# Convolution and gated two-layer network: small sums of the second layer moved between GpSimd, VectorE and DMA, and ScalarE's copies put in another order

## The chip, the core and the metric

The kernel runs on one core of a Trainium2 chip. Its engines are TensorE (PE in the profile, with PEld for its weight loads), VectorE (DVE), ScalarE (ACT), GpSimd (POOL) and SyncE (SP), each with an instruction queue of its own that is worked off in order. The metric is device time in microseconds of one execution; less is better.

## The reference

Everything is float32. A causal depthwise convolution of 7 taps over 8 sequences of 4096 tokens and 192 channels is followed by a network with 2048 hidden units and a gate:

```python
w = softmax(weight)                       # 8 heads x 7 taps
y[b, s] = sum_k w[h, k] * x[b, s - 6 + k] # 192 channels, 24 per head
h = y.reshape(32768, 192) @ w_in          # 192 x 2048
g = h * np.clip(h + 3.0, 0.0, 6.0) / 6.0
out = g @ w_out                           # 2048 x 192
```

## The kernel before

The 32768 tokens are worked off in 32 blocks of 1024. Block 0 is computed plainly at the start, together with the preparation of the weights; the other 31 run through the same two stages, `first_layer` and `second_layer`. All instructions stand in the order in which the program issues them (`tc.manual_schedule`).

**First layer.** 16 steps n = 0 to 15, two 64-row halves of TensorE's array side by side. `begin(n)` puts 12 matmuls into a slot of two PSUM banks, ScalarE scales the slot (L523), `end(n)` adds 6 matmuls, ScalarE writes relu to `g` (L302), and VectorE multiplies it with the slot (L306, a "gate"), which frees the slot. There are four slots, so `begin(n + 4)` needs gate n. Steps 0 to 7 give A11 and A22, steps 8 to 15 give A21 and A12: the tokens of a block and the hidden units are both cut in two, and these are the four quarters of the gated matrix, each 128 partitions x 8 chunks x 512 columns. Between the steps VectorE runs the convolution of a later block, `y += c[k] * x[k:]`, one instruction of 128x1536 for each tap k = 2 to 6 (L1056), before step 0 and after steps 1, 3, 5 and 7.

**Second layer.** It is a fast matrix multiplication with seven products on two levels. Level one uses the sums S3 = A11 - A21, S1 = A21 + A22 (in place of A21, by a DMA that adds, `add_pair`), S2 = S1 - A11 (in place of A11), and at the end S3 is rewritten as A12 - S2: ScalarE negates S2 into it (`negative`, L715), and a DMA adds A12. S3, S1 and the last rewriting go by pairs of chunks. Level two does the same within the products of A11, A22, A12 and S1: `small_sums` cuts a quarter into even and odd chunks and lower and upper 256 columns, x11, x12 (lower, even and odd) and x21, x22 (upper), and makes four small sums in the order 3, 2, 4 (each needs the one before it) and 1. Those of A11 lie in the tile `shared`, those of A22 in `sums4[0]` (z in the profile), those of S1 in `s5`. Form 1 of A11 and of A22 is made by two DMAs: one that copies x21 (SP's queue) and one that adds x22 (GpSimd's queue, `adding`).

The matmuls lie in four streams, one for each group of 32 columns of TensorE's array. `put` gives each a place on its stream's clock, 2 units for 512 columns and 1 for 256; each stream has 80 units. All other work of the stage gets a time on the same clock by `do(t, ...)`, and one sort by time gives the order of the program:

```python
        def do(t, fn, *args, **kw):
            streams[3].append((t - 0.5, lambda: fn(*args, **kw)))
...
        events = sorted(((t, fn) for st in streams for t, fn in st), key=lambda x: x[0])
```

So a time moved in `do` moves an instruction within its engine's queue; what it waits for is settled by the data alone. `level_two` runs one product's seven small products on one stream, in the order 1, then 6, 2, 7, 5, 4, 3, with ScalarE's copies between them (steps 1, 2, 6, 5, 7, 3 at L744 to L749): for the products of A22 on stream 2 and of A11 on stream 3 they take units 0 to 36, for that of S1 on stream 3 units 44 to 76. The rewritten S3 is used by streams 0 to 2 from unit 64 to 80, a pair of chunks every 4 units. `between` holds the preparation of the next block: `split_high` (L476), `split_low` and `split_mix` cut its convolved input into parts for the first layer.

Of the kernel before, what the change touches and what calls it, by code (L numbers as in the profile page):

```python
# [8 lines left out]
ALU = mybir.AluOpType  # L9
# [16 lines left out]
def kernel(  # L26
# [8 lines left out]
    nc = tc.nc  # L35
# [19 lines left out]
    NP = NC // 2  # L55
# [32 lines left out]
    for base, dma in ((0, nc.scalar), (D2, nc.sync)):  # L88
        dma.dma_start(
            out=w_sb[base : base + D2],  # L90
            in_=weight.unsqueeze(1).to_broadcast([H, GJ, KC]),
# [126 lines left out]
    for n in range(AHEAD):  # L218
# [8 lines left out]
        out=e_sb[:], in0=w_sb[:], in1=mx[:].to_broadcast([P, KC]), op=ALU.subtract  # L227
# [46 lines left out]
    A11, A21, A12, A22 = (g4[:, :, j] for j in range(4))  # L274
    S2, S1, S4 = A11, A21, A12
# [79 lines left out]
    every = range(NP)  # L355
# [3 lines left out]
    shared = ot.tile([P, NP, N], F32, name="shared")  # L359
# [97 lines left out]
    def add(out, x, y, op=ALU.add):  # L457
        nc.vector.tensor_tensor(out=out, in0=x, in1=y, op=op)
# [31 lines left out]
    y_own, y_other, pools, sums4 = [], [None], [], []  # L490
# [8 lines left out]
    def first_layer(i, jobs):  # L499

        slots = {}

        def both(n):
            return psum[:, 2 * slots[n] : 2 * slots[n] + 2]

        def mms(n, part, start=False, stop=False):
            group, c = divmod(n, NP)
            for s in range(K3):
                for k in range(2):
                    r = slice(k * D2, (k + 1) * D2)  # L510
                    nc.tensor.matmul(  # L511
                        out=psum[:, 2 * slots[n] + k], lhsT=r32(w_in_parts[part][r, c, s]),
                        rhs=r32(y_other[0][r, part, s] if group else y_own[part][r, s]),
                        start=start and s == 0, stop=stop and s == K3 - 1,
                        skip_group_check=True,
                    )

        def begin(n):
            slots[n] = free_slots.pop(0)
            mms(n, HIGH, start=True)  # L520
            mms(n, LOW)
            if n + 1 < count:
                nc.scalar.mul(both(n), both(n), 4097.0)  # L523
            else:
                lower, upper = (psum[:, 2 * slots[n] + k] for k in range(2))
                nc.scalar.mul(lower, lower, 4097.0)
                nc.vector.tensor_scalar(
                    out=upper, in0=upper, scalar1=4097.0, scalar2=None, op0=ALU.mult
                )

        def end(n):
            group, c = divmod(n, NP)
            mms(n, MIX, stop=True)
            to = g4[:, c, 1:3] if group else g4[:, c, 0::3]
            relu(to, both(n))
            gate(to, both(n))
            free_slots.append(slots[n])

        count = 2 * NP
        begin(0)  # L540
        begin(1)
        for job in jobs.get(-1, ()):
            job()
        for n in range(count):
            if n == count - 3:
                begin(n + 2)
            end(n)
            if n < count - 3:
                begin(n + 2)
            for job in jobs.get(n, ()):  # L550
                job()
            if n < NP and n % 2:
                small_sums(shared, A11, (3, 2, 4), nc.gpsimd, every[n - 1 : n + 1])
            if n in (3, NP - 1):
                r = slice(n - 3, n + 1)
                nc.sync.dma_start(out=four_parts(shared[:, r])[0], in_=four_parts(A11[:, r])[2])
            if n == NP - 1:
                sums4[:] = [pools[0].tile([P, NP, N], F32, name="z4", tag="own")]
                nc.sync.dma_start(out=four_parts(sums4[0])[0], in_=four_parts(A22)[2])
                small_sums(sums4[0], A22, (3,), nc.gpsimd)  # L560
                adding(four_parts(shared)[0], four_parts(A11)[3])
            if n == NP + 1:
                third_sum(0)
                add_pair(0)
                adding(four_parts(sums4[0])[0], four_parts(A22)[3])
            if n == NP + 3:
                third_sum(1)
                small_sums(sums4[0], A22, (2,), nc.gpsimd)
                add_pair(1)

    def adding(out, x):
        nc.gpsimd.dma_start(out=out, in_=x, accum_op=ALU.add)  # L572
# [8 lines left out]
    def third_sum(p, engine=nc.gpsimd):  # L581
        g_sums(engine, (3,), every[pair_of(p)], 2)
# [7 lines left out]
    def four_parts(x):  # L590
        return [x[:, c::2, t] for t in halves for c in range(2)]

    def small_sums(to, x, which, engine=nc.gpsimd, r=every):

        r = slice(r[0], r[-1] + 1)
        x11, x12, x21, x22 = four_parts(x[:, r])
        s1, s2, s3, s4 = four_parts(to[:, r])
        forms = {
            1: (s1, x21, x22, ALU.add), 2: (s2, x22, s3, ALU.subtract),
            3: (s3, x11, x21, ALU.subtract), 4: (s4, x12, s2, ALU.subtract),  # L600
        }
        for n in which:
            o, p, q, op = forms[n]
            engine.tensor_tensor(out=o, in0=p, in1=q, op=op)  # L604
# [17 lines left out]
    def second_layer(i, between):  # L622
        last = i + 1 == NB
        ours = [free_slots.pop(0) for _ in range(3)]
        x_, b, y_, c, a, _ = (psum[:, 2 * n + k] for n in ours for k in range(2))
        z = pools[1].tile([P, NP + 1, N], F32, name="z2", tag="other")
        sums2, p1 = z[:, 0:NP], z[0:DH, NP]
        ends = [psum[:, 2 * free_slots[0] + k] for k in range(2)] if last else [b, b]
        s5 = A22
        copy = nc.scalar.copy  # L630
        m = slice(0, DH)
        lo, hi = halves
        both = nc.sync, nc.scalar
        first, second, third, fourth = (rows(q) for q in range(4))
# [9 lines left out]
        clock = [0] * 4  # L644
# [5 lines left out]
        def do(t, fn, *args, **kw):  # L650
            streams[3].append((t - 0.5, lambda: fn(*args, **kw)))  # L651
# [87 lines left out]
        p4 = Fourth()  # L739

        def level_two(n, p, order, j=3):
            A, E, B, C = chains[j]
            steps = {
                1: lambda: copy(out=B, in_=A),  # L744
                2: lambda: copy(out=p()[first, lo], in_=A),
                6: lambda: copy(out=C, in_=B),
                5: lambda: copy(out=p()[second, lo], in_=E),
                7: lambda: copy(out=p()[second, hi], in_=C),
                3: lambda: copy(out=p()[first, hi], in_=C),  # L749
            }  # L750
            to = {1: A, 2: A, 6: B, 5: E, 7: C, 3: B, 4: C}
            for k in order:
                small(n, k, to[k], k in (1, 5), j)
                if k != 4:
                    do(clock[j], steps[k])

        rest = 6, 2, 7, 5, 4, 3
        chunks, first_fill = list(every), [True]
# [53 lines left out]
        assert clock == [80] * 4  # L812

        for t in halves:
            do(24 if t == hi else 20, copy, out=p4[third, t], in_=b[first, t])
        do(16, copy, out=p1[third], in_=b[second])
        do(20, copy, out=B2, in_=A2)
        do(31.9, copy, out=C2, in_=B2)
        do(32.2, copy, out=D2, in_=B2)
        do(12, copy, out=a[second], in_=a[fourth])  # L820
        do(28, copy, out=a[fourth], in_=a[second])
        do(40, lambda: copy(out=p2(second, hi), in_=C2))
        do(48, copy, out=a[second], in_=a[fourth])
        do(44, lambda: copy(out=p2(first, lo), in_=A2))
# [10 lines left out]
        do(7, small_sums, sums2, A12, (3, 2), nc.vector)  # L835
        do(7, small_sums, sums4[0], A22, (4,), nc.vector)
        do(7, small_sums, sums2, A12, (1,), nc.vector)
        for t, when in ((lo, 28.5), (hi, 32.5)):
            do(when, lambda t=t: add(S2[:, :4, t], S1[:, :4, t], A11[:, :4, t], ALU.subtract))
        do(33, small_sums, s5, S1, (3,), nc.vector)  # L840
        do(32, tiles)
        do(36, fold_with, p1)
        do(36.1, small_sums, s5, S1, (2,), nc.vector)
        do(36.2, g_sums, nc.vector, (2,), every[4:], 4)
        do(36.05, fold_with, p4, 2)
        do(38.7, copy, out=b[m], in_=p1)
        do(21, last_sum, sums2, A12)
        do(36.3, small_sums, s5, S1, (1, 4), nc.vector)
        for n, t in zip(range(0, NP, 2), (36.5, 40.5, 48.3, 50.5)):
            do(t, negative, slice(n, n + 2))  # L850
        do(45.5, lambda: copy(out=late["p7"], in_=c[m]))
        do(60.2, lambda: add(late["u3"], b[m], late["p7"]))
# [83 lines left out]
    with tc.manual_schedule():  # L936
# [4 lines left out]
            out=c_sb[:], in0=e_sb[:], in1=sm[:].to_broadcast([P, KC]), op=ALU.mult  # L941
# [14 lines left out]
        b = take()  # L956
# [62 lines left out]
        n = 3  # L1019
# [94 lines left out]
        for i in range(1, NB):  # L1114
            jobs = {n: [tap] for n, tap in zip((-1, 1, 3, 5, 7), taps)}
            jobs[-1] = left + jobs.get(-1, [])
            first_layer(i, jobs)
            def begin_conv():
                x_tiles[i + 2] = load_x(i + 2)
                conv[:] = conv_jobs(i + 2)  # L1120

            between, conv = [], []
            if i + 1 < NB:
                between += [(40, split_high), (57, split_low), (70, split_mix)]
                between += [
                    (t, lambda n=n: swap_parts(nc.gpsimd, (n,)))
                    for n, t in ((HIGH, 69), (LOW, 69), (MIX, 71))
                ]
            if i + 2 < NB:
                between += [(1, begin_conv), (58, lambda: conv[0]()), (62, lambda: conv[1]())]  # L1130
            left = second_layer(i, between)
            taps = conv[2:]
# [33 lines left out]
```

## Time and profile before

| | |
|---|---|
| median of 3 runs | 2264.55 us (2263.73 to 2266.02) |
| profiled execution | 2265.02 us, its span 2263.2 us |
| granted TensorE clock | 0.998 |
| TensorE busy | 2240.2 us (99%) |
| VectorE, ScalarE, GpSimd busy | 1938.1 us (86%), 1735.9 us (77%), 1292.1 us (57%) |
| DMA | 345.71 MB in 386540 packets, mean 153 GB/s |
| S1's adding DMAs (g<-g, L585) | 124 of 512 KB, median 6.6 us from issue to landing |
| S3's adding DMAs (s<-g) | 124 of 512 KB, median 5.6 us |
| the copies and adds of form 1 | shared<-g 62 of 256 KB by SP (2.5 us) and 31 of 512 KB by GpSimd (5.7 us); z<-g 31 of 512 KB by SP (3.2 us) and, with those of A12, 62 by GpSimd (7.3 us) |

Times in the timeline are microseconds from the start of the span. Lines of the timeline have start, length, engine, line of the program, operation, tiles (out<-in), shapes and count; an "x2" puts two instructions in a row together. What stands in brackets is the idle time before and what ended it. Spans on GpSimd are rough: an instruction can be shown as begun while the one before it still runs. The lines by stretches have, after the stretch and its length, the busy time and number of instructions of PE, PEld, DVE, ACT and POOL, then the granted clock, the DMA engines' share and GB/s. The block shown has its first layer from 1069.13 to 1102.10 and its second from 1102.10 to 1137.88; the next first layer follows until 1170.86.

### The profile page before, as it was taken

How to read it: one execution, taken by the hardware profiler on the slowest of the kernel's cores; microseconds unless marked ns; L12 is line 12 of the kernel's file. 1: busy time of each engine (PE TensorE's matmuls, PEld its weight loads, DVE VectorE, ACT ScalarE, POOL GpSimd, SP SyncE). 2: the span in 40 equal slices, each digit the busy share in tenths (PEclk: the TensorE clock that was granted, in tenths of full speed). 3: DMA queues.
4: the chain of work that ended last, by engine and by line, in shares of the span. 5: the costliest groups of instructions: out<-in, count | busy, mean ns of one | idle time of the engine just before them, and what ended most of it. 6: DMA issues, size and time to landing. Idle time of an engine off the chain costs nothing.

```text
span 2263.2 us, 55547 instructions
## 1 busy us (share of the span) xinstructions
PE 2240.2 (99%) x22984; PEld 1488.1 (66%) x22984; DVE 1938.1 (86%) x1890; ACT 1735.9 (77%) x2391; POOL 1292.1 (57%) x1064
## 2 busy tenths in 40 slices
PE   9999999999999999999999999999999999999997
PEld 6466666667666667666666666676666666666664
DVE  8888888888898888888888888888888889888875
ACT  7578787787877787877878777878778787777784
POOL 2466654566655666555666456665456655566643
PEclk9999999999999999999999999999999999999999
DMA  6388888988889878888887798787888878987776
GB/s 154 69 151 152 163 157 153 166 147 163 155 153 171 147 151 161 160 155 164 149 163 155 152 170 143 154 161 159 160 156 150 164 154 156 169 143 154 147 149 111
DMA packets 386540, 345.71 MB, mean 153 GB/s; under 512 B 213968, under 2 KB 298448, under 8 KB 386288
## 3 DMA queue, kind: packets, MB, share of 16 engines
q0 software_dynamic: 131344, 250.72, 62.1%
q1 hardware_dynamic: 253704, 91.18, 18.7%
q8 instruction: 180, 2.95, 0.5%
q14 instruction: 72, 0.59, 0.1%
q10 hardware_dynamic: 1240, 0.27, 0.1%
HBM read 31.72 MB, written 25.17 MB: 25 GB/s over the span
## 4 chain that ended last, share of the span: by engine, by line
PE 49%; POOL 16%; issue 12%; DVE 12%; DMA 7%; ACT 3%; POOLq 0%; SPq 0%; DVEq 0%; ACTq 0%
PE psum L654 25%; PE psum L511 20%; DVE g L306 7%; DMA s<-g 5%; DVE y L1056 4%; POOL s L414 4%; POOL g L572 3%; POOL z L604 2%; POOL s L572 2%; ACT g L302 2%; PE psum L296 2%; PE psum L341 2%; POOL shared L604 2%; POOL z L572 2%; DMA g<-g 1%
## 5 line engine op out<-in xcount | busy, mean ns | idle before, releaser
L654 PE MATMUL psum<-g,w_out 128*32 128x512 f32 (+1 forms) x5968 | 863.9, 505 | 7.0 <-DMA g<-g 6.1
L654 PE MATMUL psum<-s,w_out 128*32 128x512 f32 (+1 forms) x3024 | 765.9, 588 | 8.8 <-DMA s<-g 8.6
L306 DVE SCALAR_TENSOR_TENSOR g<-g,psum 128x1024 f32<-128x1024 f32 (+1 forms) x528 | 619.2, 1186 | 148.1 <-ACT g L302 147.7
L302 ACT ACTIVATE g<-psum,half 128x1024 f32<-128x1024 f32 (+1 forms) x528 | 565.2, 1087 | 5.9 <-PE psum L511 5.2
L511 PE MATMUL psum<-y_own,w_in 64*128 64x512 f32 x4464 | 523.4, 389 | 0.0
L511 PE MATMUL psum<-y_other,w_in 64*128 64x512 f32 x4464 | 516.0, 386 | 0.0
L654 PEld LDWEIGHTS psum<-g,w_out 128*32 128x32 f32 x5968 | 348.8, 109 | 243.0 <-issue 98.5
L523 ACT ACTIVATE psum<-psum 128x1024 f32<-128x1024 f32 x465 | 468.7, 1008 | 47.1 <-PE psum L511 44.9
L511 PEld LDWEIGHTS psum<-y_own,w_in 64*128 64x128 f32 x4464 | 413.5, 184 | 117.7 <-issue 26.0
L511 PEld LDWEIGHTS psum<-y_other,w_in 64*128 64x128 f32 x4464 | 418.1, 184 | 87.8
L604 POOL TENSOR_TENSOR shared<-g,shared 128x256 f32<-128x256 f32 x248 | 357.0, 1439 | 88.6 <-DVE g L306 57.1
L1056 DVE SCALAR_TENSOR_TENSOR y<-x,c_sb,y 128x1536 f32<-128x1536 f32 x186 | 335.3, 1803 | 1.5 <-ACT y L1054 1.3
L572 POOL DMA_DIRECT2D s<-g x124 | 149.4, 1264 | 283.2 <-PE psum L654 198.0
L654 PE MATMUL psum<-g,w_s 128*32 128x256 f32 x1488 | 288.3, 381 | 0.0
L654 PEld LDWEIGHTS psum<-s,w_out 128*32 128x32 f32 x3024 | 194.6, 109 | 79.2 <-DMA s<-g 19.8
L654 PE MATMUL psum<-z,w_s 128*32 128x256 f32 x992 | 232.1, 382 | 0.0
L654 PE MATMUL psum<-z,w_out 128*32 128x256 f32 x992 | 204.4, 380 | 0.0
L604 POOL TENSOR_TENSOR shared<-g 128x256 f32<-128x256 f32 x124 | 91.9, 741 | 188.6 <-DVE g L306 188.6
L414 POOL TENSOR_TENSOR s<-g 128x1024 f32<-128x1024 f32 x62 | 195.8, 3158 | 0.0
L572 POOL DMA_DIRECT2D g<-g x124 | 180.1, 1466 | 17.9 <-POOL s L414 9.1
L572 POOL DMA_DIRECT2D z<-g x62 | 94.6, 1525 | 144.7 <-ACT z L575 133.8
L651 ACT COPY psum<-psum 32x512 f32<-32x512 f32 (+1 forms) x186 | 82.9, 446 | 122.0 <-PE psum L654 118.0
(116 smaller groups left out, 2874.3 us busy)
## 6 DMA issues: line engine op xcount, KB each, us to landing
y_other<-y_own POOLq DMA_DIRECT2D x180, 384.0 KB, 8.1
g<-g POOLq DMA_DIRECT2D x124, 512.0 KB, 6.6
s<-g POOLq DMA_DIRECT2D x124, 512.0 KB, 5.6
z<-g POOLq DMA_DIRECT2D x62, 512.0 KB, 7.3
out_dram<-shared SPq DMA_DIRECT2D x378, 64.0 KB, 5.4
x<-in_x_dram SPq DMA_DIRECT2D x53, 388.5 KB, 5.7
shared<-g SPq DMA_DIRECT2D x62, 256.0 KB, 2.5
z<-g SPq DMA_DIRECT2D x31, 512.0 KB, 3.2
```

The lines of the kernel that those rows point to most:

```text
L296: nc.tensor.matmul(out=psum[:, b], lhsT=w[r], rhs=src, start=start, stop=stop, skip_group_check=onto,)
L302: nc.scalar.activation(r6, h, ACT.Relu, bias=half[:], scale=1.0 / 6.0)
L306: nc.vector.scalar_tensor_tensor(out=g_, in0=g_, scalar=1.0, in1=h, op0=ALU.min, op1=ALU.mult)
L341: lambda p=p: nc.tensor.matmul(out=bank[j * QS : (j + 1) * QS, tokens], lhsT=w_out[:, p, w, cols], rhs=x[:, p, tokens], start=(first and p ...
L414: engine.tensor_tensor(out=o[:, r], in0=a[:, r], in1=b[:, r], op=op)
L511: nc.tensor.matmul(out=psum[:, 2 * slots[n] + k], lhsT=r32(w_in_parts[part][r, c, s]), rhs=r32(y_other[0][r, part, s] if group else y_own[ ...
L523: nc.scalar.mul(both(n), both(n), 4097.0)
L572: nc.gpsimd.dma_start(out=out, in_=x, accum_op=ALU.add)
L604: engine.tensor_tensor(out=o, in0=p, in1=q, op=op)
L651: streams[3].append((t - 0.5, lambda: fn(*args, **kw)))
L654: nc.tensor.matmul(out=out, lhsT=w, rhs=x, start=start, stop=True, tile_position=(0, j * QS), skip_group_check=True,)
L1056: jobs.append(lambda k=k: nc.vector.scalar_tensor_tensor(out=y[:], in0=x[:, :, k : k + N], scalar=c_sb[:, k : k + 1], in1=y[:], op0=ALU.mu ...
```

## The change

1. First layer, GpSimd: form 1 of A11 is summed with the other three, for each pair of steps, and form 1 of A22 after step 9. The two SP copies and the two GpSimd adding DMAs that made them are dropped.
2. First layer: S3's first pair is summed by VectorE after gate 9, no longer by GpSimd.
3. Second layer, VectorE: chunks 4 and 5 of S2 are summed in two halves behind chunks 0 to 3 (times 28.6 and 32.6); only chunks 6 and 7 stay in one sum at 36.1, now ahead of form 2 of S1.
4. Second layer, ScalarE and GpSimd: the four negations with their adding DMAs go from times 36.5, 40.5, 48.3 and 50.5 to 35.6, 36.6, 41 and 45, and `split_high` from 40 to 48.4.
5. Second layer, ScalarE: seven copies that nothing needs soon go later: step 2 of the products of A11 and A22 from 20 to 28.1, the three copies out of bank b from 16, 20 and 24 to 25.5, 29 and 30, and one within bank a from 28 to 34.

```diff
             if n < NP and n % 2:
-                small_sums(shared, A11, (3, 2, 4), nc.gpsimd, every[n - 1 : n + 1])
-            if n in (3, NP - 1):
-                r = slice(n - 3, n + 1)
-                nc.sync.dma_start(out=four_parts(shared[:, r])[0], in_=four_parts(A11[:, r])[2])
+                small_sums(shared, A11, (3, 2, 4, 1), nc.gpsimd, every[n - 1 : n + 1])
             if n == NP - 1:
                 sums4[:] = [pools[0].tile([P, NP, N], F32, name="z4", tag="own")]
-                nc.sync.dma_start(out=four_parts(sums4[0])[0], in_=four_parts(A22)[2])
                 small_sums(sums4[0], A22, (3,), nc.gpsimd)
-                adding(four_parts(shared)[0], four_parts(A11)[3])
             if n == NP + 1:
-                third_sum(0)
+                third_sum(0, nc.vector)
                 add_pair(0)
-                adding(four_parts(sums4[0])[0], four_parts(A22)[3])
+                small_sums(sums4[0], A22, (1,), nc.gpsimd)
...
                 if k != 4:
-                    do(clock[j], steps[k])
+                    do(clock[j] + (8.1 if k == 2 and n != 5 else 0), steps[k])
...
         for t in halves:
-            do(24 if t == hi else 20, copy, out=p4[third, t], in_=b[first, t])
-        do(16, copy, out=p1[third], in_=b[second])
+            do(30 if t == hi else 29, copy, out=p4[third, t], in_=b[first, t])
+        do(25.5, copy, out=p1[third], in_=b[second])
...
-        do(28, copy, out=a[fourth], in_=a[second])
+        do(34, copy, out=a[fourth], in_=a[second])
...
-        for t, when in ((lo, 28.5), (hi, 32.5)):
-            do(when, lambda t=t: add(S2[:, :4, t], S1[:, :4, t], A11[:, :4, t], ALU.subtract))
+        for r, t, when in (
+            (slice(0, 4), lo, 28.5), (slice(4, 6), lo, 28.6),
+            (slice(0, 4), hi, 32.5), (slice(4, 6), hi, 32.6),
+        ):
+            do(when, lambda r=r, t=t: add(S2[:, r, t], S1[:, r, t], A11[:, r, t], ALU.subtract))
...
-        do(36.1, small_sums, s5, S1, (2,), nc.vector)
-        do(36.2, g_sums, nc.vector, (2,), every[4:], 4)
+        do(36.1, g_sums, nc.vector, (2,), every[6:], 2)
+        do(36.2, small_sums, s5, S1, (2,), nc.vector)
...
-        for n, t in zip(range(0, NP, 2), (36.5, 40.5, 48.3, 50.5)):
+        for n, t in zip(range(0, NP, 2), (35.6, 36.6, 41, 45)):
             do(t, negative, slice(n, n + 2))
...
-                between += [(40, split_high), (57, split_low), (70, split_mix)]
+                between += [(48.4, split_high), (57, split_low), (70, split_mix)]
```

## The prediction

> **What bounds the kernel now.** I read the page first, then the stretches of one steady block, then the timeline of VectorE and GpSimd in that block, the waits of TensorE's weight loads, and last the timeline of ScalarE.
>
> ```profile
> PE 2240.2 (99%) x22984; PEld 1488.1 (66%) x22984; DVE 1938.1 (86%) x1890; ACT 1735.9 (77%) x2391; POOL 1292.1 (57%) x1064
> ```
>
> The stretches of the two stages (after the length: busy time and instructions of PE, PEld, DVE, ACT, POOL):
>
> ```profile
> 1069.13:1102.10 32.97, 32.97 (x292) 26.83 (x288) 27.74 (x25) 30.90 (x32) 24.10 (x20) 1.00 0.75 159
> 1102.10:1137.88 35.78, 35.78 (x434) 19.78 (x432) 32.23 (x33) 23.24 (x43) 16.75 (x15) 1.00 0.96 157
> ```
>
> TensorE is the bound. A block is a first layer (32.97 us in every block) and a second layer (35.78 here; the blocks' period averages 69.3, so 36.3 on average). The first layer is 16 steps of 2.04 us without a gap. The second has four column groups ("streams") of 80 units each. In the timeline one unit takes 0.4293 us, so 34.4 us is its floor: at most 1.9 us per block, 58 us in all, can be won there. I placed each of its matmuls against start + 0.4293 × unit; the means of 29 blocks show where the streams fall behind: stream 3 is 0.97 late from unit 4, streams 2 and 3 are 1.22 late from unit 28, stream 3 is 1.46 late from unit 52, and all are about 2.0 late from unit 76. The waits of the weight loads (us in total, times, longest; a stretch of 29 blocks) name the causes of three: S1's first pair (unit 4), ScalarE's copies of step 7 (unit 28) and S3's negated pairs (unit 76).
>
> ```profile
> PEld psum L654 <- DMA g<-g: 22.6, 29, 1.4
> PEld psum L654 <- DMA s<-g: 16.7, 26, 1.3
> PEld psum L654 <- ACT z L748: 14.5, 29, 0.5
> ```
>
> At unit 52 the cause is ScalarE's copy of step 1 (L744, 1125.29 to 1125.63).
>
> The first layer has no wait, but VectorE has no slack there either. Start, length, engine:
>
> ```profile
> 1146.29 1.81 DVE L1056 SCALAR_TENSOR_TENSOR y<-x,c_sb,y 128x1536 f32<-128x1536 f32 x1
> 1148.02 2.43 DVE L306 SCALAR_TENSOR_TENSOR g<-g,psum 128x1024 f32<-128x1024 f32 x2
> 1150.38 1.81 DVE L1056 SCALAR_TENSOR_TENSOR y<-x,c_sb,y 128x1536 f32<-128x1536 f32 x1
> ```
>
> ```profile
> 1146.52 2.18 POOL L604 TENSOR_TENSOR shared<-g,shared 128x256 f32<-128x256 f32 x1 [1.32 <-DVE g L306]
> 1148.78 0.74 POOL L604 TENSOR_TENSOR shared<-g,shared 128x256 f32<-128x256 f32 x1
> 1149.48 0.74 POOL L604 TENSOR_TENSOR shared<-g 128x256 f32<-128x256 f32 x1
> ```
>
> A tap and two gates fill each 4.08 us. The GpSimd sum issued during a tap takes 2.18 us where its neighbours take 0.74: it ends 0.60 after the tap. The reverse is in the next lines: VectorE's sum of S3 takes 2.30 where it takes 1.21 alone (so in all 22 that I matched with a running GpSimd sum), because GpSimd's sum runs until 1106.68; 1.21 + 1.21 - 0.12 = 2.30.
>
> ```profile
> 1105.47 2.30 DVE L414 TENSOR_TENSOR s<-g 128x1024 f32<-128x1024 f32 x1
> ```
>
> ```profile
> 1103.32 3.36 POOL L604 TENSOR_TENSOR z<-g,z 128x1024 f32<-128x1024 f32 x1
> ```
>
> So a VectorE instruction with two SBUF inputs and a GpSimd sum exclude each other, whole instruction by whole instruction. Gates, which read PSUM, are not held (1.22 with GpSimd busy, 1.21 without).
>
> **The change in the first layer.** Form 1 (x21 + x22) of A11 moves to GpSimd: one more 128x256 sum per pair of steps, priced by the row of form 3 at 0.74, or 0.70 from start to start. Two SP copies and two GpSimd adding DMAs per block vanish. GpSimd then wants, from a tap's end T: form 2 to T+0.60, form 4 from T+0.68, form 1 from T+1.38, and the next pair's form 3 from T+2.08 to T+2.82. The next tap comes at T+2.28 (1150.38 against 1148.10). In before, form 3 was over 0.16 before it; now it is in its way for 0.54. No tap of before started on a running GpSimd sum (0 of 116), so this price lies between 0 and 0.54; I take 1.81 + 0.54 - 0.12 = 2.23, because the 22 sums follow it. Each pair then takes VectorE 4.51 instead of 4.08, and the second, third and fourth of the four taps end 0.42, 0.86 and 1.30 late.
>
> The Trainium skill, "SBUF — State Buffer", section "SBUF: two separate sides", says the pair of ports that VectorE and GpSimd share is locked for the whole instruction by whichever started first. By that rule the small sums hold the taps and the time is my sum; if only sums as long as those in the trace did, it would be the first rival's. The 22 waits agree with the rule.
>
> What TensorE loses: step m+4 starts in the PSUM slot that gate m frees. Gate 4 ends at 1153.31 and step 8 starts at 1153.76, 0.45 later, the same for the other even steps, 1.27 for odd ones; about 0.07 of this is latency (0.05 lie between the end of a copy, 1115.11, and the matmul that waits for it, 1115.16). Lateness of 0.42, 0.86, 1.30 against 0.38 leaves TensorE 0.04, then 0.48, then 0.92 late.
>
> S3's first pair moves to VectorE, behind gate 9. There it meets GpSimd's 2.41 us sum for A22 (form 3, L560): that one starts 2.08 after the last tap's end, the new VectorE sum is issued at 2.40. It waits 2.09, takes 1.21 + 2.09 - 0.12 = 3.18, and gate 10 ends 3.64 later than before. Against a slack of 1.27 - 0.07 + 0.92, step 14 waits 1.51 more. First layer: 32.97 + 0.92 + 1.51 = 35.4, +2.43 per block. The last block has no taps and keeps its time. Bounds: 2.0 to 2.8.
>
> Queued behind: S1's first pair (add_pair(0)) is issued by GpSimd after that sum, some 6 us before the second layer starts instead of 2.7. It landed 5.2 after its issue, so the wait at unit 4 goes even if the landing takes 2 us more. GpSimd's later sums end by 2.4 into the second layer, so VectorE's third pair there is no longer held and S1's last pairs land up to 1 us earlier. S2's pieces of 128x512 cost 0.69 each (row of 96x512; between 0.42 and 1.22), wait for S1's third pair and hide before the last pair's landing (15.4 us after the second layer's start in before), for which S1's small sums wait anyway; without that cover they would cost VectorE 1.4 and TensorE nothing, since S2's last chunks are wanted at unit 56, 24.0 us in.
>
> **The change in the second layer.** Postponing five copies before unit 28 (four of 0.36 and one of 0.58) lets step 7's copies end at 11.2 after the start instead of 13.0; unit 28 is at 12.0, so that wait goes. Then ScalarE is the limit:
>
> ```profile
> 1119.25 0.37 ACT L749 COPY z<-psum 32x256 f32<-32x256 f32 x1
> 1119.52 1.05 ACT L575 ACTIVATE s<-g 128x1024 f32<-128x1024 f32 x1
> 1120.60 0.59 ACT L651 COPY psum<-z 96x512 f32<-96x512 f32 x1
> 1121.21 0.36 ACT L822 COPY shared<-psum 32x256 f32<-32x256 f32 x1
> 1121.60 1.49 ACT L476 ACTIVATE y_own<-y 128x1536 fp32r<-128x1536 f32 x1
> 1122.99 1.05 ACT L575 ACTIVATE s<-g 128x1024 f32<-128x1024 f32 x1
> 1123.94 0.34 ACT L824 COPY shared<-psum 32x256 f32<-32x256 f32 x1
> 1124.29 0.36 ACT L825 COPY shared<-psum 32x256 f32<-32x256 f32 x1
> 1124.68 0.59 ACT L851 COPY shared<-psum 96x512 f32<-96x512 f32 x1
> 1125.29 0.34 ACT L744 COPY psum<-psum 32x256 f32<-32x256 f32 x1
> ```
>
> S3's first negation now runs ahead of the L749 copies, which so end at 17.5 as in before, though TensorE is there 1.2 earlier. From there to L744 come negations two, three and four (3 × 1.05) and copies of 0.59, 0.36, 0.34, 0.36 and 0.59: 5.4 us, and with L744 23.2. Before it was 5.8 and 23.5, with split_high's 1.49 in place of two negations. Unit 52 (22.32) waits until 23.2: stream 3 is 0.87 late instead of 1.46. The copy into bank b makes streams 0 to 2 wait 0.2 to 0.5 at unit 44, less than that. The negations' adding DMAs go through GpSimd's queue, which sat idle for 2.0 to 4.9 us between them in before. The last negation goes out at 22.1 instead of 26.0, and its landing (7.5 in before) at 29.6 is 3 us ahead of unit 76: that 0.54 goes. Gain: 2.0 - 0.87 = 1.13 per block; bounds 0.5 (an ACT queue 0.6 longer) to 1.7 (lateness of 0.3).
>
> **Sum.** 30 × 2.43 = 73 lost, 30 × 1.13 + 2 for the last block = 36 gained. The profiled execution took 2265.0 (span 2263.2 and 1.8 around it), 0.5 above the median of 2264.55. 2264.5 + 37 = 2301.5 is the median that I expect. With the bounds, 2275 to 2334.
>
> **Rivals.** First, faster: the sums never get ahead of a tap, and GpSimd falls behind instead. It decides on 0.20 us: form 3 of the second pair is issued at 1150.18, the tap at 1150.38. Then S3's first pair meets a 0.74 sum at most and gate 10 ends 0.85 late, within its 1.20; the first layer stays at 33.0. The wait at unit 4 may stay, but its 0.97 lies beside unit 52's 0.87, so some 33 are gained: 2232. For it: no tap was ever held. Against it: the two engines' mutual waits above, and that a tap and four sums (1.7 + 2.8) exceed 4.08. Second: the taps are held, but S3's first pair gets in ahead of the 2.41 us sum (0.32 us decide). Then only 0.92 is lost: 30 × 0.92 - 36 = -8: 2257, between 2241 and 2277 by the bounds of the second layer. Third: GpSimd runs two sums in a row before a waiting tap gets its turn, and each of three taps waits 0.7 more: 30 × 2.1 = 63 more, 2365; nothing in the trace shows it.
>
> **How the numbers follow.** My forecast 0.65, the first rival 0.15, the second 0.13, the third 0.05, others 0.02. The range from 2245 to 2334 takes in the forecast with its bounds and nearly all of the second rival and leaves 0.2 out. A measurement of this kernel tells about 0.2% (4.5 us) from no change. Faster: the first rival and two thirds of the second, 0.24; same 0.07; slower 0.69.
>
> **What would show it.** Right: a first layer of about 35.4 us and a second of about 35.2; taps of 2.2 us; a VectorE sum at L414 of about 3.2 behind gate 9; no wait for DMA g<-g at unit 4 or DMA s<-g at unit 76. Wrong: taps still at 1.81 and a first layer of 33.0, or a second layer whose lateness at unit 52 is not ScalarE's.

## The result and the profile after

The changed kernel takes 2327.3 us (2325.49 to 2328.69) beside 2264.1 us before: a ratio of 1.0277, 95% interval 1.0259 to 1.0295. It is 63 us slower. The prediction said 2301.5, slower with a chance of 0.69, and a range of 2245 to 2334. The profiled execution took 2328.69 us, with a span of 2326.9.

The first line of the profile's page of the kernel after, to be held against that of before:

```profile
PE 2266.4 (97%) x22984; PEld 1474.6 (63%) x22984; DVE 2031.7 (87%) x1983; ACT 1738.2 (75%) x2391; POOL 1292.0 (56%) x1126
```

VectorE has 93 instructions and 94 us more, GpSimd 62 instructions more and the same busy time; DMA moves 280.66 MB instead of 345.71. Then the stretches of one block of the kernel after, first and second layer (stretch, length, busy time and count of PE, PEld, DVE, ACT, POOL, clock, DMA share, GB/s):

```profile
1099.69:1134.94 35.25, 34.01 (x290) 26.53 (x289) 31.65 (x26) 30.87 (x32) 25.93 (x23) 1.00 0.52 112
1134.94:1171.09 36.15, 35.87 (x434) 19.52 (x432) 31.60 (x35) 23.34 (x43) 14.79 (x15) 1.00 0.79 133
```

From the first matmul of one layer to that of the next, as a mean over the blocks, before has 32.97 and 36.33 us, after has 35.26 and 36.16. So the first layer loses 2.29 per block and the second wins only 0.17; 30 × 2.12 = 64 is the whole difference.

The waits of the weight loads in the kernel after (what waited for what: us in total, times, longest):

```profile
PEld psum L511 <- DVE g L306: 79.2, 113, 1.6
...
PEld psum L649 <- ACT psum L646: 21.4, 29, 0.7
PEld psum L649 <- ACT shared L740: 21.4, 28, 0.8
PEld psum L649 <- ACT psum L739: 16.1, 29, 0.6
```

The first line is new: TensorE's first-layer steps wait for gates. The waits for S1's first pair, for S3's pairs and for step 7's copies, which led this list before, are gone. In their place stand three waits for ScalarE (L646, L739 and L740 are L651, L744 and L745 of before), at units 44, 52 and 64.

Now one first layer of the kernel after. VectorE's timeline (start, length):

```profile
1116.52 2.26 DVE L1054 SCALAR_TENSOR_TENSOR y<-x,c_sb,y 128x1536 f32<-128x1536 f32 x1
...
1125.51 3.26 DVE L414 TENSOR_TENSOR s<-g 128x1024 f32<-128x1024 f32 x1
```

GpSimd's timeline beside it:

```profile
1115.72 1.45 POOL L599 TENSOR_TENSOR shared<-g 128x256 f32<-128x256 f32 x2
...
1125.29 2.40 POOL L599 TENSOR_TENSOR z<-g 128x1024 f32<-128x1024 f32 x1
1129.07 1.24 POOL L567 DMA_DIRECT2D g<-g  x1 [1.38 <-DVE s L414]
```

The first GpSimd line is form 1 and the next pair's form 3. They run until 1117.17, and the tap shown at 1116.52 takes 2.26 instead of 1.81. The second is A22's sum: it began 0.22 ahead of VectorE's sum for S3, which then takes 3.26. GpSimd's end, 1127.69, plus VectorE's own 1.23 is 1128.92; the sum ends at 1128.77. The last line issues the DMA for S1's first pair, 5.9 us before the second layer starts.

### The profile page after: what moved, and what is told of

Read it like the earlier page. It is cut to its first block, busy times and chain, and to the rows that moved or that the text cites. A ratio compares the mean times of both kernels' runs of the same rounds, so it can differ in the third digit from the quotient of the medians.

```text
span 2326.9 us, 55119 instructions
## 1 busy us (share of the span) xinstructions
PE 2266.4 (97%) x22984; PEld 1474.6 (63%) x22984; DVE 2031.7 (87%) x1983; ACT 1738.2 (75%) x2391; POOL 1292.0 (56%) x1126
## 2 busy tenths in 40 slices
DMA packets 320570, 280.66 MB, mean 121 GB/s; under 512 B 211489, under 2 KB 232481, under 8 KB 320321
## 4 chain that ended last, share of the span: by engine, by line
PE 40%; DVE 25%; ACT 24%; issue 10%; DMA 0%; POOL 0%; SPq 0%; DVEq 0%; ACTq 0%
PE psum L649 25%; DVE g L306 14%; PE psum L511 11%; DVE y L1054 8%; ACT s L570 5%; ACT g L302 3%; ACT psum L646 3%; ACT psum L523 2%; DVE y_own L1077 2%; ACT y L1052 2%; PE psum L296 2%; PE psum L341 2%; ACT y_own L476 2%; ACT shared L646 1%; ACT shared L740 1%
## 5 line engine op out<-in xcount | busy, mean ns | idle before, releaser
L649 PE MATMUL psum<-s,w_out 128*32 128x512 f32 (+1 forms) x3024 | 721.5, 589 | 0.0
L306 DVE SCALAR_TENSOR_TENSOR g<-g,psum 128x1024 f32<-128x1024 f32 (+1 forms) x528 | 604.8, 1180 | 73.0 <-ACT g L302 72.7
L511 PE MATMUL psum<-y_other,w_in 64*128 64x512 f32 x4464 | 546.2, 393 | 38.4 <-DVE g L306 35.2
L1054 DVE SCALAR_TENSOR_TENSOR y<-x,c_sb,y 128x1536 f32<-128x1536 f32 x186 | 372.1, 2000 | 1.5 <-ACT y L1052 1.4
L599 POOL TENSOR_TENSOR shared<-g 128x256 f32<-128x256 f32 x248 | 179.9, 742 | 179.6 <-DVE g L306 179.6
L649 PE MATMUL psum<-z,w_out 128*32 128x256 f32 x992 | 227.3, 379 | 0.0
L567 POOL DMA_DIRECT2D g<-g x124 | 166.6, 1362 | 82.0 <-DVE s L414 82.0
L266 POOL DMA_DIRECT2D y_other<-y_own x90 | 48.0, 534 | 284.4 <-issue 264.9
L649 PEld LDWEIGHTS psum<-g,w_s 128*32 128x32 f32 x1488 | 132.5, 109 | 98.3 <-ACT shared L740 22.1
L649 PEld LDWEIGHTS psum<-s,w_out 128*32 128x32 f32 x3024 | 179.4, 109 | 21.2
L646 ACT COPY psum<-psum 32x512 f32<-32x512 f32 (+1 forms) x186 | 82.9, 446 | 124.3 <-PE psum L649 121.1
```

The lines of the kernel that those rows point to most:

```text
L266: dma.dma_start(out=to[D2:P], in_=part[0:D2])
L306: nc.vector.scalar_tensor_tensor(out=g_, in0=g_, scalar=1.0, in1=h, op0=ALU.min, op1=ALU.mult)
L511: nc.tensor.matmul(out=psum[:, 2 * slots[n] + k], lhsT=r32(w_in_parts[part][r, c, s]), rhs=r32(y_other[0][r, part, s] if group else y_own[ ...
L649: nc.tensor.matmul(out=out, lhsT=w, rhs=x, start=start, stop=True, tile_position=(0, j * QS), skip_group_check=True,)
L1054: jobs.append(lambda k=k: nc.vector.scalar_tensor_tensor(out=y[:], in0=x[:, :, k : k + N], scalar=c_sb[:, k : k + 1], in1=y[:], op0=ALU.mu ...
```

## Experiments

All were compared with the kernel before on the same chip. The last two columns are the mean lengths of first and second layer, as above.

| kernel | us | ratio to before, 95% | first | second |
|---|---|---|---|---|
| before | 2264.1 to 2265.9 | | 32.97 | 36.33 |
| after | 2327.3 | 1.0259 to 1.0295 | 35.26 | 36.16 |
| e1_first_only | 2306.7 | 1.0165 to 1.0196 | 35.27 | 35.44 |
| e2_second_only | 2285.2 | 1.0072 to 1.0102 | 32.97 | 37.04 |
| e3_sum_gpsimd | 2301.8 | 1.0145 to 1.0176 | 33.78 | 36.81 |
| e4_form1_dma | 2276.4 | 1.0035 to 1.0069 | 33.51 | 36.30 |
| e5_a22_behind | 2284.8 | 1.0075 to 1.0105 | 33.76 | 36.23 |
| e6_y_later | 2313.3 | 1.0200 to 1.0230 | 35.26 | 35.69 |
| e9_old_second | 2241.0 | 0.9879 to 0.9908 | 32.97 | 35.47 |
| e8_best | 2227.6 | 0.9821 to 0.9854 | 32.97 | 35.14 |
| e11_neg_only | 2326.9 | 1.0260 to 1.0294 | 35.26 | 36.24 |
| e10_split_earlier | 2213.7 | 0.9761 to 0.9790 | 32.97 | 34.67 |

**The two halves of the change.** e1_first_only is the kernel before with the first layer's part of the change (points 1 and 2 of the list above) and nothing else; e2_second_only is the kernel after with that part undone.

> The kernel before with the first layer's part of the change alone (all small sums of A11 and A22 on GpSimd, third_sum(0) on VectorE); the second layer stays as before. Theory A (GpSimd's sums and VectorE's sums hold each other): the first layer is 2.28 us longer per block as in the kernel after, taps 2.2 us and third_sum(0) 3.2 us; the wait at unit 4 goes and part of the one at unit 76, worth 0.2 to 0.7 a block: 2312 to 2326. Rival, the loss of the kernel after sits in the second layer's new order: near 2264 or below it.

> The kernel after with the first layer of before; S2 in pieces and the new order of ScalarE's copies stay. Theory A: the first layer is back at 33.0 us, the wait at unit 4 (0.97 us) is back, but later waits of 1.2 and 1.7 us on ScalarE set the lag anyhow: 2256 to 2264. Rival, the gain that the prediction gave to the second layer (1.13 a block) is there when the first layer doesn't disturb it: about 2230.

The halves add up: in the first layer +2.30 and 0, in the second -0.89 and +0.71, together -0.18 where the kernel after shows -0.17. So the first-layer half makes the first layer longer and the second shorter, since S1's first pair lands before it is wanted: no wait for it is left in e1_first_only. The reordering of the second layer is a loss by itself, some 20 us. For e1 the first layer came as expected, but the time lies 5 us below the range, because the second layer gains 0.89 per block where I had put 0.2 to 0.7. For e2 neither theory held: I had thought that the wait at unit 4 would be covered by the later waits for ScalarE, and it was not. Measured against start + 0.4293 × unit, the most delayed stream of e2 is late by 0.97 from unit 4, 1.39 from unit 44, 2.07 from unit 52 and 2.56 from unit 64; in the kernel after by 0.05, 0.52, 1.20 and 1.68. Nearly the same steps come on top of the lateness that is there. ScalarE is late too in e2: `split_high`, which matters at unit 64, starts 24.8 us into the stage, in the kernel after 24.0.

**What in the first layer costs 2.29.** Three kernels, each the kernel after with one edit. e3_sum_gpsimd:

```diff
-                third_sum(0, nc.vector)
+                third_sum(0)
```

> The kernel after with S3's first pair (third_sum(0)) back on GpSimd. Theory A: the taps are still held by GpSimd's sums (2.2 us), so about 0.7 us a block is left of the 2.28, and the S1 pair lands some 2 us later, which may cost 0.2 to 0.5 at unit 4: 2279 to 2293. Theory B (VectorE is simply full, and its added 1.2 us sum is the loss): the whole loss but what the second layer gains goes, about 2259.

e4_form1_dma:

```diff
-                small_sums(shared, A11, (3, 2, 4, 1), nc.gpsimd, every[n - 1 : n + 1])
+                small_sums(shared, A11, (3, 2, 4), nc.gpsimd, every[n - 1 : n + 1])
+            if n in (3, NP - 1):
+                r = slice(n - 3, n + 1)
+                nc.sync.dma_start(out=four_parts(shared[:, r])[0], in_=four_parts(A11[:, r])[2])
...
                 small_sums(sums4[0], A22, (3,), nc.gpsimd)
+                adding(four_parts(shared)[0], four_parts(A11)[3])
```

> The kernel after with A11's first small sums (form 1) taken by a copy and an adding DMA again, as before; the A22 sum on GpSimd and third_sum(0) on VectorE stay. GpSimd begins A22's sum about 2.3 us earlier, so that third_sum(0) meets less of it. Theory A (exclusion, the form-1 sums get in ahead of a tap): the taps are 1.8 us again and their lateness (0.7) goes, third_sum(0) falls from 3.26 to some 2.5: first layer 33.4 us, 2265 to 2280. Theory B (VectorE's added sum alone): no change from after, 2327.

e5_a22_behind:

```diff
-                small_sums(sums4[0], A22, (3,), nc.gpsimd)
             if n == NP + 1:
                 third_sum(0, nc.vector)
                 add_pair(0)
+                small_sums(sums4[0], A22, (3,), nc.gpsimd)
                 small_sums(sums4[0], A22, (1,), nc.gpsimd)
```

> The kernel after with GpSimd's form-3 sum of A22 (2.4 us) issued behind add_pair(0) instead of just before VectorE's third_sum(0). Theory A (third_sum(0) is long because it meets that sum): third_sum(0) takes 1.2 us again, step 14's wait of 1.5 us goes, only the taps' lateness of 0.7 is left in the first layer (33.7 us): about 2280. Theory B (VectorE's added 1.2 us is the loss, wherever GpSimd is): no change, 2327.

The groups of the taps and of VectorE's S3 sums (L414; after "|" busy time and mean ns of one) tell them apart. First e4_form1_dma:

```profile
L1058 DVE SCALAR_TENSOR_TENSOR y<-x,c_sb,y 128x1536 f32<-128x1536 f32 x186 | 335.2, 1802 | 1.5 <-ACT y L1056 1.4
L414 DVE TENSOR_TENSOR s<-g 128x1024 f32<-128x1024 f32 x93 | 148.6, 1625 | 1.1
```

Then e5_a22_behind:

```profile
L1054 DVE SCALAR_TENSOR_TENSOR y<-x,c_sb,y 128x1536 f32<-128x1536 f32 x186 | 371.8, 1999 | 1.5 <-ACT y L1052 1.3
```

Without form 1 on GpSimd, every tap is as before (1802 ns; 1803 before) and steps 8, 10 and 12 start on time; with it they stay held (1999; 2000 in the kernel after). The sum for S3 behind gate 9 takes what is left of A22's sum in front of it, in VectorE's timelines of e4_form1_dma and of e5_a22_behind:

```profile
1102.67 2.48 DVE L414 TENSOR_TENSOR s<-g 128x1024 f32<-128x1024 f32 x1
```

```profile
1105.89 1.23 DVE L414 TENSOR_TENSOR s<-g 128x1024 f32<-128x1024 f32 x1
```

In e4 A22's sum started at 1101.66, 1.01 ahead, and the first layer is 0.54 longer than before. In e5 the two no longer meet, and 0.79 is left, that of the taps. So of the 2.29, form 1 on GpSimd costs about 0.8 by holding the taps, and the meeting with A22's sum adds 1.5. The two aren't independent: without form 1 the meeting costs only 0.54, because A22's sum then starts 1.01 instead of 0.22 ahead, and VectorE's sum takes 2.48 instead of 3.26. Theory B is refuted: VectorE makes the same added sum in e4 and e5. The time of e4 lies in its range, that of e5 is 5 us above the 2280 expected. For e3 the first layer is as expected (+0.81), the time is 9 us over the range: S1's first pair, issued 2.8 us later than in the kernel after, costs more, with a mean lateness of 0.51 from unit 4 and another 0.59 at unit 44, where the kernel after has 0.41. Why the step at unit 44 is larger there is not shown.

**A first layer in which nothing meets.** e9_old_second is the kernel before with two edits:

```diff
-                small_sums(sums4[0], A22, (3,), nc.gpsimd)
...
-                third_sum(0)
+                third_sum(0, nc.vector)
                 add_pair(0)
+                small_sums(sums4[0], A22, (3,), nc.gpsimd)
```

> The kernel before with two edits in the first layer alone: third_sum(0) on VectorE, GpSimd's form-3 sum of A22 behind add_pair(0); all DMAs of the small sums stay. By the first runs the early add_pair(0) is worth 0.83 us a block and the sums cost something only where they meet: first layer 33.0, second layer 34.9, about 2239. Theory B (VectorE has no room for the added sum): first layer later by 0.5 to 1.2, 2255 to 2275.

The first layer stays at 32.97 with the added sum on VectorE (1.23 us), and the early pair brings 0.86 in the second: the ratio is 0.9893, 24 us faster. All the DMAs of before are still there (345.71 MB), so it isn't the smaller traffic that makes the second layer shorter.

**What in the second layer costs 0.71.** e6_y_later is the kernel after with `conv[0]`, the next block's first y multiply on ScalarE, at another time:

```diff
-                between += [(1, begin_conv), (58, lambda: conv[0]()), (62, lambda: conv[1]())]
+                between += [(1, begin_conv), (60.3, lambda: conv[0]()), (62, lambda: conv[1]())]
```

> The kernel after with the next block's first y multiply moved from due time 58 to 60.3, behind step 2's copy of the last product. If unit 64's wait (0.45 us in stream 3) comes from the chain split_high (moved to 48.4), split_low on VectorE, y multiply, that copy: the second layer is 0.4 shorter in each block, about 2313. Rival, ScalarE is late there for other reasons and the wait moves to the next unit: 2325 to 2327.

The chain is seen in ScalarE's timeline of the kernel after. Its second layer starts at 1134.94, so unit 52 is due at 1157.26 and unit 64 at 1162.42:

```profile
1158.04 0.34 ACT L739 COPY psum<-psum 32x256 f32<-32x256 f32 x1
...
1158.89 1.48 ACT L476 ACTIVATE y_own<-y 128x1536 fp32r<-128x1536 f32 x1
...
1162.19 1.58 ACT L1052 ACTIVATE y<-x,c_sb 128x1536 f32<-128x1536 f32 x1 [1.46 <-DVE y_own L1077]
1163.68 0.35 ACT L740 COPY shared<-psum 32x256 f32<-32x256 f32 x1
```

L739 is the copy that stream 3 waits for at unit 52; it ends at 1158.38. `split_high` (L476), moved behind it, ends at 1160.37; VectorE's `split_low` (1160.40 to 1162.16) had to wait for it; the y multiply waits for that, with ScalarE idle for 1.46; and behind the multiply stands the copy that TensorE wants. With the multiply moved, the wait for L740 is missing from the list, 0.47 per block and 14 us are won, as expected.

e8_best joins the first layer of e9_old_second with the second layer of the kernel after, mended on ScalarE:

```diff
-        do(38.7, copy, out=b[m], in_=p1)
+        do(40.1, copy, out=b[m], in_=p1)
...
-        for n, t in zip(range(0, NP, 2), (35.6, 36.6, 41, 45)):
+        for n, t in zip(range(0, NP, 2), (35.6, 40.2, 41, 48.2)):
...
-        do(45.5, lambda: copy(out=late["p7"], in_=c[m]))
+        do(48.3, lambda: copy(out=late["p7"], in_=c[m]))
...
-                between += [(1, begin_conv), (58, lambda: conv[0]()), (62, lambda: conv[1]())]
+                between += [(1, begin_conv), (60.3, lambda: conv[0]()), (62, lambda: conv[1]())]
```

> First layer as before but with third_sum(0) on VectorE and A22's form-3 sum behind add_pair(0), so that nothing meets; second layer as after, with ScalarE's order mended: copy b[m]<-p1 from 38.7 to 40.1, negations at 35.6, 40.2, 41, 48.2 instead of 35.6, 36.6, 41, 45, the p7 copy at 48.3, the y multiply at 60.3. If first layer and second layer are independent, as the first runs say (the early add_pair(0) is worth 0.83 a block, the new ScalarE order costs 0.72 through units 44, 52 and 64): first layer 33.0, second layer 34.3 to 34.9, 2215 to 2235. Rival, the new order costs its 0.72 through something else than these copies: 2257 to 2264.

The time is within the forecast, the second layer 0.2 above its part of it (35.14 against 34.3 to 34.9). Its greatest lateness is 0.19 up to unit 58 and 0.70 at the end. To see whether these mends are worth something each, e11_neg_only takes only the first three pieces of that diff into the kernel after.

> The kernel after with only ScalarE's earlier order mended (copy b[m]<-p1 at 40.1, negations at 35.6, 40.2, 41, 48.2, the p7 copy at 48.3), the y multiply left at 58. The waits at units 44 and 52 (0.43 and 0.65) go. If the copy behind the y multiply lands at the same absolute time as in the kernel after (split_high, split_low, y multiply, copy: done near 29.1), unit 64 swallows what was gained: second layer 35.4 to 35.7, 2320 to 2328. Rival, the waits add up, and each mend is worth its own size: second layer 34.6, about 2295.

The lateness at units 44 and 52 is gone (0.14 up to unit 58), and from unit 64 it is 1.74, where the kernel after has 1.68. Both kernels give the same time. The waits of e11_neg_only:

```profile
PEld psum L649 <- ACT shared L740: 27.9, 28, 1.0
...
PEld psum L649 <- DVE shared L458: 19.9, 28, 0.7
```

`split_high` stands behind the same work on ScalarE in both, starts 24.0 us into the stage in both, and the copy ends at about 29.1. What is won at units 44 and 52 is lost again in front of this chain, so their mends pay only together with that of unit 64: with the latter alone (e6_y_later) the second layer has 35.69, with all of them (e8_best, with another first layer) 35.14. The second line is the next one in the row: VectorE's fold of the last product, which stands behind `split_low`. It is what e8_best is left with:

```profile
PEld psum L654 <- DVE shared L458: 20.6, 29, 0.7
```

e10_split_earlier is e8_best with two more times changed:

```diff
-        do(48.3, lambda: copy(out=late["p7"], in_=c[m]))
+        do(48.05, lambda: copy(out=late["p7"], in_=c[m]))
...
-                between += [(48.4, split_high), (57, split_low), (70, split_mix)]
+                between += [(48.1, split_high), (57, split_low), (70, split_mix)]
```

> The last kernel (e8_best) with ScalarE's split_high at 48.1 and the p7 copy at 48.05, both ahead of the last negation (48.2). In e8_best all that is left of the second layer's lag is 0.55 us at unit 64, where TensorE waits for VectorE's fold of the last product, which stands behind split_low, which waits for split_high. If so, split_low ends at 26.3 instead of 27.3 and the 0.55 goes: second layer 34.1, 2211 to 2215. Rival, the fold waits for TensorE's own product by then, or the later negation delays the last S3 pair (due at unit 76): 2222 to 2228.

That wait is gone too, and the lateness at the stage's end is 0.23. The stretches of one block of this kernel:

```profile
1046.12:1079.09 32.97, 32.97 (x291) 26.83 (x289) 29.21 (x27) 30.89 (x32) 23.31 (x21) 1.00 0.81 172
1079.09:1113.90 34.81, 34.81 (x434) 20.80 (x432) 31.15 (x34) 23.20 (x43) 15.23 (x15) 1.00 0.90 149
```

At 2213.7 us it beats both kernels, the one before by a ratio of 0.9775 (0.9761 to 0.9790). It moves 345.72 MB by DMA, as much as before.

## Why the prediction was right, and where it was off

- The taps: 2.23 predicted; 2.17, 2.25 and 2.24 in the last three of the four. The S3 sum: 3.18 predicted, 3.26 measured. Steps 8, 10 and 12 are 0, 0.32 and 0.67 late (forecast 0.04, 0.48 and 0.92), and step 14 waits 1.48 more (1.51). The first layer was to lose 2.43 per block and loses 2.29. This term holds, and e4, e5 and e9 show its two parts.
- The Trainium skill, "SBUF — State Buffer", section "SBUF: two separate sides", has the first starter hold the shared ports for its whole instruction. The trace agrees: A22's sum started 0.22 earlier and VectorE's waited until its end. No gate, with one input in PSUM, was held: 1180 ns on average after, 1186 before.
- The first rival, that the sums never get ahead of a tap, failed on the 2.25 us taps; the second, that S3's sum gets in first, on 3.26. The third, two sums in a row ahead of a tap, would need taps of 2.9.
- S1's first pair is issued 5.9 us before the second layer and lands 0.8 before its start (2.7 before and 2.5 after its start in the kernel before). The wait at unit 4 is gone, as forecast, and VectorE's third pair takes 1.22, no longer 2.29.
- The second layer is where a step failed: "Gain: 2.0 - 0.87 = 1.13 per block" measured 0.17, below the term's own bound of 0.5, and the second layer of about 35.2 us that was named as a sign did not come (36.16). I took unit 52 for the last wait that counts. Its lateness is 1.20, not 0.87: the copies at L744 end at 17.7 instead of 17.5, and L739, which begins 5.4 later as forecast, ends at 23.4. And I costed the move of `split_high` only by the 1.49 that it takes out of the way, not by who waits for it: `split_low`, the y multiply, the copy L740, and unit 64, where another 0.48 is added. The final lateness is 1.7, not 0.87.
- So of the 26 us between 2301.5 and 2327.3, the second layer makes 30 × 0.96 = 29, the first layer gives back 30 × 0.14 = 4. That 2327.3 still lies in the range is in part luck: the upper end had room for a first layer that loses 2.8, and it lost 2.29. Added up, the terms' bounds also give 2271.5 to 2331.5, not 2275 to 2334.
- I had also put the gain in the wrong half. The prediction credits the reordering together with the early pair; e1 and e2 show the early pair at -0.89 and the reordering at +0.71.

## What to carry to other kernels

Before work is moved between GpSimd and VectorE, lay both queues side by side: what counts is which GpSimd instruction is in front when VectorE issues one with two SBUF inputs, and how long it still runs; putting the same sum behind the other engine's turn brought the loss here from 2.29 us per block to 0.79. When an instruction is postponed to clear a queue, follow its readers to the end, over every engine, and cost the last one. Late places along one queue aren't worth their sizes one by one: mend the last one first, then look again.

## What was not expected of the hardware

How little decides the order: form 3 was shown to begin 0.1 to 0.2 us ahead of the tap that it holds for 0.44, A22's sum 0.22 ahead of one that it holds for 2. And S1's first pair takes 5.1 us from issue to landing in the kernel after, which moves 65 MB less by DMA (19%), and 5.2 before, where it is issued 3.2 us later. That doesn't mean that the traffic counts for nothing: in e4_form1_dma and e9_old_second, where the pair is issued as early as in the kernel after and the DMAs of A11's form 1 are there, it takes 7.1 and 7.4 and lands 1.2 and 1.1 us after the second layer's start, still ahead of unit 4 (1.7). Which of the transfers delays it is not shown.
